# A spectral layer with a routed expert layer on one core: where the next batches' rows are loaded and split, which engine subtracts, and how many buffers the weight parts have

## The chip, the cores and the metric

The kernel runs on one core of a Trainium2 chip. Its engines run at the same time, each through its own queue of instructions in order: TensorE multiplies matrices (PE in the profile, PEld its weight loads), VectorE (DVE), ScalarE (ACT) and GpSimd (POOL) work on tiles, and SyncE (SP) issues transfers between the memory of the chip and the core's own buffers. GpSimd issues the indirect transfers, which send each row to an address that another tile holds. Engines wait for each other through semaphores.

The metric is the time of one execution on the device in microseconds (us), as the median of several runs. Less is better.

## The reference

What is computed, cut to what matters (B = 8 sequences of S = 2496 rows with D = 256, then N = 19968 rows, 8 experts, F = 1024):

```python
X = np.fft.rfft(x, axis=1)
Yr = Xr @ w_r - Xi @ w_i + b_r
Yi = Xr @ w_i + Xi @ w_r + b_i
Y = shrink(Yr, 0.01) + 1j * shrink(Yi, 0.01)     # sign(v) * max(|v| - 0.01, 0)
y = np.fft.irfft(Y, n=2496, axis=1)

x = y.reshape(N, D)
logits = x @ w_gate + modality_bias[modality_id]
e_idx = argmax(logits); gate_w = softmax(logits)[e_idx]
for e in range(8):
    out[e_idx == e] = gate_w * (relu(x @ w1[e]) @ w2[e])
```

## The kernel before

The Fourier transform of length 2496 = 39 x 64 is done in two stages as matrix products, and so is its inverse. To keep enough digits, most operands are split in a high part (rounded) and a low part (the rest), and a product takes three multiplications: high by high, high by low, low by high.

A **batch** is one of the 8 sequences, and `build` (L984) runs them one after the other with hand-written order on TensorE, ScalarE, VectorE and GpSimd (`manual_schedule`, L993). SP is not in that list: the order of the transfers that SP issues is made by a planner from its own estimate of times, under the dependences of the code. A transfer whose buffer isn't free yet holds SP's queue.

A batch has two parts:

- **Ten pairs** (`for p in range(10)`, L1074). Each pair takes two of the 20 frequencies k1 through the second stage (`s2_pair`, L278), the mixing with w_r and w_i (`mix_sums`, L315), the shrinking (`shrink`, L324) and the first stage of the inverse (`is2_pair`, L333). In pair i the loads of pair i+4 are issued (`a_load`, L271), `s2_pair` runs for i+2, mixing and shrinking for i+1 and `is2_pair` for i. ScalarE copies the bias into the accumulator that the next pair's mixing adds to (`mix_bias`, L301).
- **The pivot stage** (`for j in range(J)`, J = 22, L1140): `pivot` (L354) and `is1` (L370) end the inverse and give the rows and their logits. ScalarE and VectorE take turns in copying is1's result (L376, L1148).

Beside these four other jobs are threaded through the same queues:

- **The first stage of batch b+2.** Its rows come in six groups u of four columns (`s1_load`, L209; three transfers on SP each, L226), the tile "x" with **two** buffers. A group gives two chunks c of 512 columns (the last group one): `s1_split` (L231) rounds a chunk to its high part (L240, on ScalarE from batch 2 on) and subtracts to get its low part (L241, on GpSimd for c < 6 from batch 2 on, on VectorE otherwise). `s1_split` also issues the load of its own and of the next group where that hasn't been done. The parts have six buffers each. Groups 0 and 1 are loaded at pairs 2 and 3 (L1102), chunks 0 to 5 are split at the ends of pairs 4 to 9 (L1129), chunks 6 to 10 in the pivot stage (L1145). `s1_chunk` (L244) multiplies them, all in the pivot stage, ScalarE copies the result (L261) and SP stores it to a scratch tensor (L266) that the next batches' `a_load` reads. In batch 0 the same is done for batches 0 and 1 at the start.
- **Routing** of batch b-1's rows (`route`, L456): some twenty small operations, most on VectorE, a few per pair in pairs 0 to 5.
- **Sends** of batch b-1's rows to their experts' regions (`scatter`, L534): 22 indirect transfers of GpSimd, four at each of pairs 6 to 9 (L1107), then one per pivot.
- **The expert weights' parts** (`SplitWeights`, L947): 64 pieces. A `step` (L968) rounds a piece on ScalarE (L977, tile "wh"), subtracts (L978, tile "wl", GpSimd in the pairs and VectorE in the pivot stage), stores both (L979, L980) and loads the next piece (L962, L965, tile "wr" with two buffers). "wh" and "wl" come from the pool w1 and have **one** buffer each. From batch 1 on there is a step in each of pairs 0 to 5 (L1104), in batch 0 in pairs 3 to 7, and at two to four places of each pivot stage (L1150).

Batches 6 and 7 prepare no further batch, and their pivot stages have no chunks.

After the batches `Experts.run` (L901) multiplies the sorted rows in tiles of 256 with their expert's weights (`ffn`, L788); `load_x` and `load_w` bring a tile's rows and weights. Its memory overlays that of the batches.

Of the kernel before, what the change touches and what calls it, by code (L numbers as in the profile page):

```python
# [9 lines left out]
F32 = mybir.dt.float32  # L10
# [13 lines left out]
D = 256  # L24
# [5 lines left out]
P1 = 3 * N1  # L30
# [97 lines left out]
class Attn:  # L128
# [5 lines left out]
    def pools(self, ctx):  # L134
        tc, nb = self.tc, self.nb
        pool = lambda name, bufs, **k: ctx.enter_context(tc.tile_pool(name=name, bufs=bufs, **k))
        self.cp = pool("consts", 1)
        self.w3 = pool("w3", 3)
        self.w4 = pool("w4", 4)

        pool("wq", 1).tile([128, 32], F32, name="wqad")
        self.w6 = pool("w6", 6)
        self.w2 = pool("w2", 2)
        self.w1 = pool("w1", 1)
        self.cl = pool("cl", 1)
        self.ps = pool("ps", 2, space=PSUM)
        self.dr = pool("dr", 2, space=DRAM)
        self.scr = [None] * nb
        self.xt, self.xs = {}, {}
# [59 lines left out]
    def s1_load(self, b, u, end=None, eng=None):  # L209

        nc = self.nc
        eng = eng or nc.sync
        end = end or u + 1
        n = min(4 * end, J) - 4 * u
        xv = self.I["x"][b].rearrange("(a c) d -> a c d", c=N2)
        if b == 0 and u < 5 or b == 1 and u < 3:

            if u == 0:
                self.early = self.x1f[0] if b else self.w1.tile([128, 2 * N2, K1, 2], F32, tag="z", name="x_0")
                if not b:  # L220
                    self.early = self.early.rearrange("p n k r -> p (n k r)")
            xt = self.early[:P1, u * 4 * D:end * 4 * D].rearrange("p (j d) -> p j d", d=D)
        else:
            xt = self.w2.tile([P1, 4, D], F32, tag="x", name=f"x_{b}_{u}")
        for g in range(3):
            ins = eng.dma_start(xt[g * N1:(g + 1) * N1, :n, :], xv[:, GB[g] + 4 * u:GB[g] + 4 * u + n, :])  # L226
        for v in range(u, end):
            self.xt[b, v] = xt[:, 4 * (v - u):4 * (v - u) + 4, :]
        return ins

    def s1_split(self, b, c):  # L231
        nc = self.nc
        u, h = c // 2, c % 2
        for v in (u, u + 1):
            if v < 6 and (b, v) not in self.xt:
                self.s1_load(b, v)
        x = self.xt[b, u][:, 2 * h:2 * h + 2, :].rearrange("p j d -> p (j d)")
        xh = self.w6.tile([P1, 512], F32R, tag="x1h", name=f"x1h_{b}_{c}")
        xl = self.w6.tile([P1, 512], F32R, tag="x1l", name=f"x1l_{b}_{c}")
        (nc.vector.tensor_copy if b == 1 or b == 0 and c % 2 == 0 else nc.scalar.copy)(xh, x)  # L240
        (nc.gpsimd if b > 1 and c < 6 else nc.vector).tensor_sub(xl, x, xh)  # L241
        self.xs[b, c] = xh, xl

    def s1_chunk(self, b, c, ahead):  # L244
# [739 lines left out]
def build(tc, I, out, nb):  # L984
    nc = tc.nc
    with ExitStack() as outer:
        dp = outer.enter_context(tc.tile_pool(name="wsp", bufs=1, space=DRAM))
        wsp = dp.tile([E * 128, 8192], F32, name="wsp")
        with ExitStack() as ctx:
            at = Attn(tc, I, nb)  # L990
            rt = Route(outer, tc, I, at, nb)
            at.pools(ctx)
            ctx.enter_context(tc.manual_schedule(engines={ET.PE, ET.Activation, ET.DVE, ET.Pool}))  # L993
            sw = SplitWeights(tc, I, at.w2, at.w1, wsp)
            at.x1f.append(at.cl.tile([128, J * GC], F32, name="x1b"))
            ld, xs, bs, ss = {}, {}, {}, {}
            last = 10 * nb
# [1 line left out]
            def load(i):  # L999
                if i < last:  # L1000
                    ld[i], ins = at.a_load(*divmod(i, 10))
                    return ins

            def s2(i):
                if i < last:
                    xs[i] = at.s2_pair(*divmod(i, 10), ld.pop(i))
# [13 lines left out]
            def bias(i):  # L1020
                if i < last:
                    bs[i] = at.mix_bias(*divmod(i, 10))

            def ahead(i):
                load(i + 4)
                s2(i + 2)
# [45 lines left out]
            for b in range(nb):  # L1072
                done = b == nb - 1
                for p in range(10):  # L1074
                    i = 10 * b + p
                    due = state == "pe"

                    apart = b == nb - 2 and p == 9
                    if b == 0:
                        if p % 2 == 0 and p < 8:  # L1080
                            with tc.issue_after(ins.ins):
                                if p < 6:
                                    at.table_load("m", p // 2 + 2)
                                at.table_load("q", p // 2 + 1)
                        ins = load(i + 4)
                        s2(i + 2)
                        if p == 0:
                            sw.load()
                            sw.load()
                        if p == 3:  # L1090
                            late = [rt.consts(), at.consts_last()]
                        if p in (3, 6):
                            for g in late:
                                next(g, None)
                        for c in (2 * p + ahead1, 2 * p + ahead1 + 1):
                            if c < 11 and nb > 1:
                                at.s1_chunk(1, c, 2)
                    elif p > 0:
                        ahead(i)
                    if p == 1:  # L1100
                        rt.load_ids(b)
                    if p in (2, 3) and b + 2 < nb:  # L1102
                        at.s1_load(b + 2, p - 2)
                    if p < 6 if b > 0 else 2 < p < 8:  # L1104
                        sw.step(nc.gpsimd)
                    if p > 5:
                        rt.scatter(4)  # L1107
                    if done and 4 < p < 9:
                        bias(i + 2)
                    ending = i == last - 2  # L1110
                    if ending:
                        mix_last(i + 1, 0)
                    else:
                        mix(i + 1, 0 if apart else None)
                    if p < 9 and not (done and p > 4):
                        bias(i + 2)
                    if due:
                        state = next(routing, None)
                    at.is2_pair(b, p, ss.pop(i))
                    if apart:  # L1120
                        mix(i + 1, 1)
                    if ending:
                        mix_last(i + 1, 1)
                    for _ in range(3):
                        if state != "pe":
                            state = next(routing, None)
                    if p == 8:
                        rt.bias(b)
                    if p > 3 and b + 2 < nb:  # L1129
                        at.s1_split(b + 2, p - 4)  # L1130
                if b != nb - 2:
                    for _ in routing:
                        pass

                s1 = [(b + 2, c) for c in range(11)] if b + 2 < nb else []
                if s1:
                    at.s1_chunk(*s1.pop(0), 0)
                    at.s1_chunk(*s1.pop(0), 0)
                pend = []
                for j in range(J):  # L1140
                    rt.scatter(1)
                    pend.append((j, at.pivot(b, j)))
                    chunk = j % 2 == 1 and j != 15
                    if len(s1) > 4 and chunk:
                        at.s1_split(*s1[4])  # L1145
                    if len(pend) > 2:
                        jj, r = pend.pop(0)
                        at.is1(b, jj, *r, nc.scalar.copy if done or jj % 2 else nc.vector.tensor_copy)  # L1148
                    if j in (8, 18) or (b == 0 and j == 13) or (b == nb - 2 and j in (3, 13)):
                        sw.step(nc.vector)  # L1150
                    if s1 and chunk:
                        at.s1_chunk(*s1.pop(0), 0)
                    next(routing, None)
                for _ in routing:
                    pass
                bias(10 * b + 11)
                ahead(10 * b + 10)
                for jj, r in pend:
                    at.is1(b, jj, *r, nc.scalar.copy)
                routing = rt.route(b)  # L1160
                if b == nb - 3:
                    rt.setup_pads()
                    routing = chain(routing, rt.tiles_early())
                if b == nb - 2:
                    rt.fence()
# [38 lines left out]
```

## Time and profile before

| | us |
|---|---|
| median of three runs | 1585.96 |
| lowest and highest of them | 1584.24, 1587.04 |
| the profiled execution's own time | 1588.58 |
| its span, from the first to the last instruction | 1586.8 |
| from the start to the end of the last batch's pivot stage | 667.5 |

The profile is of one execution. A line of the view by groups or of the timeline has the kernel's line (L240 is line 240), the engine, the operation, the tile that is written and those that are read ("x1h<-x"), and their shapes. In the timeline the first two numbers are the start and the duration in us, and what stands in brackets is the idle time of the engine ahead of the instruction, with what ended it. In the view of waits a row has the engine and line that waited, what it waited for, and the total, the number and the longest of these waits in us. In the view by stretches a row has the stretch, its length, the busy time of PE, PEld, DVE, ACT and POOL with their instructions, the granted share of TensorE's clock, the busy share of the DMA engines and GB/s. SPq rows are transfers that SP issues: how long the issue took, not the transfer.

In the profiled execution batch 1 runs its pairs from 143.4 to 186.2 us and its pivot stage to 219.9, and a pair takes 4.5 to 4.9 us.

### The profile page before, as it was taken

What the parts mean: (1) busy time and instruction counts of PE and PEld (TensorE: products, weight loads), DVE (VectorE), ACT (ScalarE), POOL (GpSimd) and SP (SyncE); (2) the same over time, 40 slices, a digit from 0 to 9 for tenths busy, and PEclk for the clock granted to TensorE, in tenths of its full rate; (3) what the DMA queues carried; (4) which work ended last, traced back from release to release, by engine and by line L of the source; (5) the groups of instructions that cost most, each with busy time, mean ns of one, the idle gap of its engine ahead of it and who ended that gap; (6) DMA issues with size and microseconds to landing.
All of it is one profiled execution on the core that took longest, in us unless ns stands there. A gap on an engine that the chain in (4) does not pass through costs nothing. (4 is left out here: it accounts for less than half of the span.)

```text
span 1586.8 us, 34903 instructions
## 1 busy us (share of the span) xinstructions
PE 1510.0 (95%) x12459; PEld 1479.4 (93%) x12459; DVE 695.8 (44%) x1460; ACT 660.9 (42%) x1345; POOL 563.5 (36%) x548
## 2 busy tenths in 40 slices
PE   4889999999999999889999999999999999999998
PEld 2889898989898999889999999999999999999998
DVE  3555555555565666434333333333333333233332
ACT  2466565656565655522323323232233323232232
POOL 0031727272727262523643232222223222222232
PEclk8999999999999999999999999999999999999999
DMA  7866676767676665552442423752225228635541
GB/s 205 260 210 222 200 228 200 229 201 226 203 232 199 214 185 187 149 184 55 99 119 55 150 45 63 244 159 43 52 44 159 45 42 262 233 67 161 146 133 45
DMA packets 290201, 244.44 MB, mean 154 GB/s; under 512 B 208586, under 2 KB 243990, under 8 KB 286207
## 3 DMA queue, kind: packets, MB, share of 16 engines
q1 hardware_dynamic: 271033, 200.60, 43.6%
q0 software_dynamic: 18992, 41.58, 8.0%
q8 instruction: 100, 1.64, 0.4%
q14 instruction: 76, 0.62, 0.1%
HBM read 432.70 MB, written 100.08 MB: 336 GB/s over the span
## 5 line engine op out<-in xcount | busy, mean ns | idle before, releaser
L833 PE MATMUL y<-w,hh 128*128 128x256 f32 x2496 | 437.0, 278 | 7.4 <-DMA w<-wsp 6.9
L803 PE MATMUL h<-xh,w 128*128 128x256 f32 x2496 | 403.5, 278 | 5.1 <-DMA w<-wsp 5.1
L833 PEld LDWEIGHTS y<-w,hh 128*128 128x128 f32 x2496 | 379.3, 188 | 8.3 <-issue 7.0
L833 PE MATMUL y<-w,hl 128*128 128x256 f32 x1248 | 347.5, 278 | 0.1
L803 PEld LDWEIGHTS h<-xh,w 128*128 128x128 f32 x2496 | 339.8, 189 | 5.4 <-issue 5.4
L846 POOL DMA_INDIRECT out<-o,ix x161 | 158.5, 984 | 440.4 <-ACT o L825 402.8
L806 DVE SCALAR_TENSOR_TENSOR hl<-h,hh 128x512 fp32r<-128x512 f32 x312 | 209.5, 689 | 228.6 <-ACT hh L805 225.0
L803 PE MATMUL h<-xl,w 128*128 128x256 f32 x1248 | 245.3, 278 | 0.0
L805 ACT ACTIVATE hh<-h 128x512 fp32r<-128x512 f32 x312 | 178.3, 596 | 152.7 <-PE h L803 152.7
L833 PEld LDWEIGHTS y<-w,hl 128*128 128x128 f32 x1248 | 234.8, 188 | 0.6 <-DVE hl L806 0.3
L321 PE MATMUL mx<-wmix,Xh 128*128 128x256 f32 x1280 | 183.6, 287 | 6.1 <-ACT mx L301 6.1
L803 PEld LDWEIGHTS h<-xl,w 128*128 128x128 f32 x1248 | 189.4, 189 | 0.0
L825 ACT ACTIVATE o<-y,xt 128x256 f32<-128x256 f32 x78 | 37.1, 476 | 347.6 <-PE y L833 347.6
L823 DVE TENSOR_SCALAR o<-y,xt 128x256 f32<-128x256 f32 x78 | 37.8, 484 | 327.3 <-ACT o L825 322.9
L321 PEld LDWEIGHTS mx<-wmix,Xh 128*128 128x128 f32 x1280 | 163.5, 192 | 6.8 <-ACT mx L301 6.3
L783 POOL TENSOR_TENSOR xl<-tr,xh 128x512 fp32r<-128x512 f32 x78 | 100.9, 1294 | 192.8 <-ACT xh L782 192.8
L978 POOL TENSOR_TENSOR wl<-wr,wh 128x512 fp32r<-128x512 f32 x47 | 60.4, 1285 | 253.8 <-ACT wh L977 180.3
L361 PE MATMUL pv<-pv,z 128*120 128x136 f32 x704 | 113.5, 287 | 3.0 <-DVE pl L367 2.5
L361 PEld LDWEIGHTS pv<-pv,z 128*120 128x120 f32 x704 | 101.9, 190 | 10.1 <-DVE pl L367 2.7
L367 DVE TENSOR_TENSOR pl<-pv,ph 120x264 fp32r<-120x264 f32 x176 | 75.3, 431 | 66.5 <-ACT ph L366 62.6
L330 DVE SCALAR_TENSOR_TENSOR s<-mx,u 128x512 f32<-128x512 f32 (+1 forms) x81 | 55.5, 685 | 106.2 <-ACT u L329 106.2
L321 PE MATMUL mx<-wmix,Xl 128*128 128x256 f32 x640 | 101.2, 281 | 0.0
(186 smaller groups left out, 2065.8 us busy)
## 6 DMA issues: line engine op xcount, KB each, us to landing
w<-wsp SPq DMA_DIRECT2D x166, 2048.0 KB
a<-scr SPq DMA_DIRECT2D x80, 256.0 KB
xt<-xs SPq DMA_DIRECT2D x624, 32.0 KB
scr<-ev SPq DMA_DIRECT2D x112, 160.0 KB
x<-in_x SPq DMA_DIRECT2D x108, 156.0 KB
wr<-in_moe_w SPq DMA_DIRECT2D x64, 256.0 KB
wsp<-wh SPq DMA_DIRECT2D x64, 256.0 KB
wsp<-wl SPq DMA_DIRECT2D x64, 256.0 KB
```

The lines of the kernel that those rows point to most:

```text
L321: self.nc.tensor.matmul(ps[i][:, i, :], t[:, 2 * i + c, o:o + 128], self.w[:, wi, c, lo, :], start=False, stop=n == len(ops) - 1, skip_gro ...
L330: nc.vector.scalar_tensor_tensor(s, ps, LAM, u, ALU.add, ALU.min)
L361: nc.tensor.matmul(ps[:PK, c * 128:c * 128 + D // 2 + E], self.z[:, o:o + 3, :, :].rearrange("p n k r -> p (n k r)"), self.pv[:, c, :], st ...
L367: nc.vector.tensor_sub(pl, ps[:PK, :GC], ph)
L783: nc.gpsimd.tensor_sub(xl, tr, xh)
L803: nc.tensor.matmul(ps[:, q, :], w1[:, lo, c, f * 128:(f + 1) * 128], x[:, c, :], start=n == 0, stop=n == 5)
L805: nc.scalar.activation(hh[:, 2 * p:2 * p + 2, :], ps, AF.Relu)
L806: nc.vector.scalar_tensor_tensor(hl[:, 2 * p:2 * p + 2, :], ps, 0.0, hh[:, 2 * p:2 * p + 2, :], ALU.max, ALU.subtract)
L823: nc.vector.tensor_scalar_mul(o[:, s, :], y[s], gate)
L833: nc.tensor.matmul(y[s], lhsT, w2[:, lo, f, :], start=n == 0, stop=n == 23)
L846: ins = self.nc.gpsimd.indirect_dma_start(out=self.out, out_offset=bass.IndirectOffsetOnAxis(ap=ix, axis=0), in_=o, in_offset=None, bounds ...
L978: eng.tensor_sub(lo, raw, hi)
```

## The change

The tile "x" moves to a pool of its own with three buffers. All six groups of batch b+2 are loaded at fixed pairs, 1, 2, 3, 5, 7 and 9, and chunks 0 to 5 are split at the ends of pairs 3 to 8, one pair earlier each. Every low part (L241) is VectorE's. Pairs 6 to 9 issue three sends each instead of four; the others follow one per pivot as before. "wh" and "wl" come from the pool w2 and have two buffers each.

```diff
@@ pools
         self.w6 = pool("w6", 6)
+        self.wx = pool("wx", 3)
         self.w2 = pool("w2", 2)
@@ s1_load
-            xt = self.w2.tile([P1, 4, D], F32, tag="x", name=f"x_{b}_{u}")
+            xt = self.wx.tile([P1, 4, D], F32, tag="x", name=f"x_{b}_{u}")
@@ s1_split
         (nc.vector.tensor_copy if b == 1 or b == 0 and c % 2 == 0 else nc.scalar.copy)(xh, x)
-        (nc.gpsimd if b > 1 and c < 6 else nc.vector).tensor_sub(xl, x, xh)
+        nc.vector.tensor_sub(xl, x, xh)
@@ build
-            sw = SplitWeights(tc, I, at.w2, at.w1, wsp)
+            sw = SplitWeights(tc, I, at.w2, at.w2, wsp)
@@ build, the pairs
                     if p == 1:
                         rt.load_ids(b)
-                    if p in (2, 3) and b + 2 < nb:
-                        at.s1_load(b + 2, p - 2)
+                    if p in (1, 2, 3, 5, 7, 9) and b + 2 < nb:
+                        at.s1_load(b + 2, (1, 2, 3, 5, 7, 9).index(p))
                     if p < 6 if b > 0 else 2 < p < 8:
                         sw.step(nc.gpsimd)
                     if p > 5:
-                        rt.scatter(4)
+                        rt.scatter(3)
...
                     if p == 8:
                         rt.bias(b)
-                    if p > 3 and b + 2 < nb:
-                        at.s1_split(b + 2, p - 4)
+                    if 2 < p < 9 and b + 2 < nb:
+                        at.s1_split(b + 2, p - 3)
```

## The prediction

> **What bounds the kernel now.** The first page gives the span and the busy engine; the view of waits then says what TensorE (PE) waits for.
>
> ```profile
> span 1586.8 us, 34903 instructions
> PE 1510.0 (95%) x12459; PEld 1479.4 (93%) x12459; DVE 695.8 (44%) x1460; ACT 660.9 (42%) x1345; POOL 563.5 (36%) x548
> ...
> PE i L373 <- ACT x L376: 12.8, 4, 5.1
> ...
> PE i L373 <- ACT x1b L376: 8.7, 5, 4.1
> ...
> PE mx L321 <- ACT mx L301: 6.1, 1, 6.1
> PE pv L361 <- DVE pl L367: 2.5, 1, 2.5
> ...
> ACT x1h L240 <- DMA x<-in_x: 30.0, 7, 5.8
> ```
>
> TensorE is the bound, so only its idle time and its slow time can be won: 1586.8 - 1510.0 = 76.8 us idle. 12.8 + 8.7 = 21.5 us of it stand before L373, the first product of is1, behind a ScalarE copy (L376). That copy isn't slow: the last row says that ScalarE itself waited 30.0 us, in seven places, for rows of x. I read one of these places in order of time, in batch 1's pivot stage (TensorE, then ScalarE, GpSimd, SP).
>
> ```profile
> 190.68 0.40 PE L256 MATMUL s<-x1h,c_f 117*120 117x512 f32 x1
> ...
> 193.04 0.40 PE L256 MATMUL s<-x1h,c_f 117*120 117x512 f32 x1
> ...
> 198.89 0.57 PE L373 MATMUL i<-ph,c_g 120*117 120x264 f32 x1 [3.69 <-ACT x L376]
> ...
> 199.69 0.63 PE L256 MATMUL s<-x1h,c_f 117*120 117x512 f32 x1
> ...
> 204.10 0.63 PE L256 MATMUL s<-x1h,c_f 117*120 117x512 f32 x1
> ...
> 197.94 0.62 ACT L240 CAST x1h<-x 117x512 fp32r<-117x512 f32 x1 [4.44 <-DMA x<-in_x]
> ...
> 197.17 1.27 POOL L241 TENSOR_TENSOR x1l<-x,x1h 117x512 fp32r<-117x512 f32 x1
> ...
> 192.82 1.40 SPq L226 DMA_DIRECT2D x<-in_x  x3
> ...
> 198.47 1.16 SPq L226 DMA_DIRECT2D x<-in_x  x3
> ```
>
> Group 4's load leaves SP at 192.82, and its first half is rounded (L240) only at 197.94. ScalarE stands 4.44 us, is1's copies queue behind it, and TensorE idles 3.69. The two x buffers explain the lateness: the sixth load leaves at 198.47, just after GpSimd ends a low part at 197.17 + 1.27 = 198.44. GpSimd gets to that part late, behind its sends.
>
> The stall is paid twice. Two pivots with one chunk take 193.04 - 190.68 = 2.36 us ahead of it and 204.10 - 199.69 = 4.41 right after: slow time loses (4.41 - 2.36) / 4.41 = 46%. The view by stretches, over the six stages that prepare a later batch, shows the granted clock:
>
> ```profile
> 108.47:140.83 32.36, 29.32 (x197) 27.00 (x197) 18.64 (x42) 22.26 (x55) 1.28 (x1) 0.95 0.66 207
> 186.17:219.92 33.75, 30.06 (x197) 27.78 (x197) 17.81 (x41) 22.62 (x54) 17.20 (x17) 0.90 0.72 223
> ...
> 501.87:534.65 32.78, 28.89 (x197) 26.76 (x197) 17.69 (x41) 22.16 (x54) 17.28 (x19) 0.95 0.65 200
> sum 199.26, PE 175.76 PEld 162.50 DVE 107.58 ACT 134.06 POOL 87.21; mean PE 29.29 PEld 27.08 DVE 17.93 ACT 22.34 POOL 14.54
> ```
>
> The third number from the end is the clock: 0.95 in four stages, 0.90 in two, and full or half between. Half clock thus filled 2 x (0.05 x 4 + 0.10 x 2) x 33.2 = 26.6 us (33.2 is 199.26 / 6), and 46% of it, 12.2 us, is lost.
>
> **The change part by part.** *Loads, third buffer, earlier splits.* All six loads of a batch are issued by pair 9, groups 3 to 5 two pairs after the preceding one or two; each needs a buffer whose low parts VectorE ended in the pair before. Group 4 leaves in pair 7, three pairs ahead of the pivots that use it, where it left in their midst. The same 18 transfers move per batch, none is added. I take the stalls before L373 as gone, with their slow time: 21.5 + 12.2 = 33.7 us. The bounds are that, and nothing.
>
> *Low parts on VectorE.* From the groups by line, the ones that VectorE does already:
>
> ```profile
> L241 DVE TENSOR_TENSOR x1l<-x,x1h 117x512 fp32r<-117x512 f32 x52 | 36.6, 707 | 30.9 <-ACT x1h L240 29.1
> ```
>
> Six of each of six batches, 36 subtractions, leave GpSimd and add 36 x 0.707 = 25.5 us to VectorE's queue, in pairs 3 to 8, each between a pair's last routing operation and the next pair's L290. Is there room? Pairs 4 and 5 of batch 1:
>
> ```profile
> 162.97 0.59 ACT L301 COPY mx<-bias 128x512 f32<-128x512 f32 x1
> ...
> 163.82 1.19 PE L321 MATMUL mx<-wmix,Xh 128*128 128x256 f32 x8
> ...
> 163.71 0.68 DVE L348 COPY z<-zs 128x512 f32<-128x512 f32 x1
> ...
> 165.75 0.63 DVE L290 TENSOR_TENSOR Xl<-s,Xh 128x512 fp32r<-128x512 f32 x1
> ...
> 166.41 0.39 ACT L291 ACTIVATE Xh<-s 128x256 fp32r<-128x256 f32 x1 [1.72 <-DVE Xl L290]
> 166.69 0.61 ACT L977 CAST wh<-wr 128x512 fp32r<-128x512 f32 x1
> 167.20 0.69 ACT L329 ACTIVATE u<-mx,nlam 128x512 f32<-128x512 f32 x1
> 167.78 0.60 ACT L301 COPY mx<-bias 128x512 f32<-128x512 f32 x1
> ...
> 168.44 1.20 PE L321 MATMUL mx<-wmix,Xh 128*128 128x256 f32 x8
> ```
>
> This is a closed chain: routing after L348 holds L290 until 165.75, L291 waits for it, then L977, L329 and L301 follow without a break, and L321 starts 0.06 us after L301 ends (168.38). A pair earlier the margin is 163.82 - 163.56 = 0.26. A low part, 0.65 us from start to next start, shifts pair 4's chain past it by 0.4, and pair 5's chain by a second 0.65, so TensorE loses about 0.4 + 0.9 = 1.3 us per batch, in batches 1 to 5: 6.5 us. From pair 6 on there is neither L977 nor routing ahead of L290, and the addition hides. Each loss is under 1 us, and the shortest of the stalls above that has half clock in its stage is 2.5 (L361, stage 0, clock 0.95), so I add no slow time. I take 6.5; the ends are 0 and 25.5 (each low part on the path). ScalarE's own roundings only move one pair forward.
>
> *Two buffers for wh and wl.* Two ScalarE waits hang on a store of the single buffer:
>
> ```profile
> 82.13 0.62 ACT L977 CAST wh<-wr 128x512 fp32r<-128x512 f32 x1 [7.21 <-DMA wsp<-wh]
> ...
> 134.73 0.62 ACT L977 CAST wh<-wr 128x512 fp32r<-128x512 f32 x1 [2.77 <-DMA wsp<-wh]
> ...
> 76.99 0.38 SPq L979 DMA_DIRECT2D wsp<-wh  x1
> ...
> 77.89 0.45 SPq L962 DMA_DIRECT2D wr<-in_moe_w  x1
> ...
> 75.00:91.00 16.00, 9.88 (x67) 9.69 (x66) 3.73 (x7) 5.30 (x10) 3.82 (x3) 0.79 0.71 241
> ```
>
> The second makes the 2.5 us before L361. Its store is then two pieces back: gone, 2.5 us (its slow time is in the 26.6 above). The first makes the 6.1 before L321, and the clock of 0.79 over 16 us adds 2 x 0.21 x 16 = 6.7 us of half clock, 3.1 lost: 9.2 in all. Not all is won: the third piece, one pair (168.44 - 163.82 = 4.6 us) later, needs raw weights that leave SP at 77.89. At the store's own 82.13 - 76.99 = 5.1 us they land at 83.0. ScalarE would want them at 82.13 - 7.21 + 4.6 = 79.5: a wait of 3.5. As 7.21 of ScalarE's wait cost 6.1 of TensorE, 1.1 is hidden: 2.4 remain, and a slow stretch as in the last stage (2 x 0.05 x 32.78 = 3.3 us, 46% of it) 1.5. I take 9.2 - 3.9 = 5.3; the ends are 0 and 9.2.
>
> *Sends.* The 22 sends stay, 12 of them in pairs 6 to 9 instead of 16. GpSimd, freed of the low parts, ends them no later in batches 1 to 5; in 6 and 7, where it had none, a few us later. Expert tile 0's second weights must follow the last send, but stand in SP's queue behind four tiles' row loads: 0.
>
> *The sum.* 33.7 + 2.5 + 5.3 - 6.5 = 35.0 us. The profiled execution took 1588.58 around its 1586.8, so it would take 1553.6; the median of the runs, 1585.96, becomes 1551.
>
> **A rule that speaks against it.** Sends ran beside VectorE's low parts already:
>
> ```profile
> 191.69 0.69 DVE L241 TENSOR_TENSOR x1l<-x,x1h 117x512 fp32r<-117x512 f32 x1
> ...
> 191.86 1.41 POOL L536 DMA_INDIRECT xs<-x1b,si  x1 [0.19 <-issue]
> 193.58 0.99 POOL L536 DMA_INDIRECT xs<-x1b,si  x1 [0.30 <-issue]
> ```
>
> The low part kept its 0.69, the send took 1.41 instead of 0.99. The Trainium skill, "SBUF — State Buffer", section "SBUF: two separate sides", says that a VectorE operation with two SBUF inputs takes the port shared with GpSimd for its whole length, and whoever starts second blocks. By that rule the trace's 0.42 of lengthening is the send's; with the send first, VectorE would wait.
>
> **The rivals.**
> - *The chain has cover* (the margin grows as ScalarE runs ahead): the 6.5 is 0, and 1585.96 - 41.5 = 1544. For it: VectorE is 44% busy. Against: 0.06 us of margin.
> - *The next wait ends just as late.* A load stands behind stores in SP's queue, which is ordered by the planner's own estimate of times, or the last group arrives late: half of 33.7 stays, 1568. For it: 192.82 above was such a queue place. Against: the loads now leave pairs earlier.
> - *VectorE waits for GpSimd's port.* In pairs 5 to 8 sends run back to back. If each of four low parts waits a whole 0.99 and hides half, 6 batches x 4 x 0.5 = 12 us: 1563. Against: the 0.69 above.
> - *SP blocks (slower).* Loads of groups 3 to 5 wait at SP's head for a low part, and scratch loads (L275) stand behind them:
>
> ```profile
> 173.34 4.91 SPq L275 DMA_DIRECT2D a<-scr  x2
> 183.33 1.91 SPq L226 DMA_DIRECT2D x<-in_x  x3
> ```
>
>  Already here SP stands from 178.25 to 183.33, 5.1 us, and TensorE doesn't stall. L275 loads four pairs ahead and is used two pairs later, 9.2 us; with 5.1 to land, 4.1 are free by this estimate. Blocks of 6.9 us (one and a half pairs) would cost 2.8 each, 18 of them 50 us: 1601. It is slower than before from 4.1 + 35.0 / 18 = 6.0 us per block.
> - *The loads stay late*, since SP's order is the planner's and not the code's: only 2.5 + 5.3 - 6.5 = 1.3 is left, 1585.
>
> **How the numbers follow.** Forecast 0.52, cover 0.20, next wait 0.13, port 0.07, loads stay 0.04, SP blocks 0.04. The likeliest gives 1551. The range takes in the cover with the start's whole 9.2 (1541) and reaches over the half-kept stall to the chain's upper end (1551 + 25.5 - 6.5 = 1570); it leaves out the last two cases and some tails. About 0.2%, 3 us, is what a measurement of this kernel can tell from no change. Faster 0.92, same 0.04 (the loads stay), slower 0.04.
>
> **What would show it.** Right: no wait of L373 for L376 above 1 us in stages 0 to 5, their clock at 1.00 and each near 27 us; no L241 on GpSimd; L321 waiting some 0.4 to 0.9 us for L301 in pairs 5 and 6 of batches 1 to 5; the stall at 77.8 shorter, a pair later. Wrong: L240 still waiting for x in the pivots, L284 waiting for the scratch loads, or pairs 4 to 9 longer than 4.6 us throughout.

## The result and the profile after

| | before | after |
|---|---|---|
| median of the runs, us | 1585.96 | 1552.01 |
| lowest and highest | 1584.24, 1587.04 | 1549.88, 1552.37 |
| ratio, with its 95% interval | | 0.978 (0.9764 to 0.9796) |
| the profiled execution's span | 1586.8 | 1550.2 |
| its six pivot stages that prepare a batch | 199.26 | 162.10 |
| its pairs of batches 1 to 5, from pair 0 to pair 9 | 41.62 to 41.74 each | 42.08 to 42.25 each |
| its pairs of batch 0, likewise | 51.96 | 51.59 |

The change makes the kernel 2.2% faster, 1 us from the forecast of 1551. All lines from 143 on are one higher in the changed kernel (L373 is L374, L240 is L241), and one higher again in the kernels below that have a third buffer for the raw weights. First its page, and then its view of waits, with the rows that answer to those shown of before.

```profile
span 1550.2 us, 34912 instructions
PE 1498.1 (97%) x12459; PEld 1468.4 (95%) x12459; DVE 712.4 (46%) x1496; ACT 659.6 (43%) x1345; POOL 517.9 (33%) x512
```

```profile
PEld mx L322 <- ACT mx L302: 7.7, 11, 5.2
...
PE mx L322 <- ACT mx L302: 5.0, 1, 5.0
...
ACT x1h L241 <- DMA x<-in_x: 3.4, 1, 3.4
...
PE i L374 <- ACT x1b L377: 0.3, 2, 0.2
...
PE i L374 <- ACT x L377: 0.2, 1, 0.2
```

TensorE's 21.5 us ahead of is1 have become 0.5, and ScalarE waits 3.4 us for rows of x where it waited 30.0. No row is left of L362 (before's L361) waiting for "pl". The stretches of the six stages, cut as in the prediction:

```profile
106.54:133.59 27.05, 27.05 (x198) 25.24 (x197) 18.62 (x42) 22.07 (x54) 0.00 (x0) 1.00 0.63 202
179.39:206.40 27.01, 27.01 (x197) 25.23 (x197) 17.90 (x41) 21.80 (x53) 13.75 (x13) 1.00 0.76 236
...
471.09:498.09 27.00, 27.00 (x198) 25.23 (x197) 17.92 (x41) 21.76 (x53) 14.18 (x15) 1.00 0.66 200
sum 162.10, PE 162.10 PEld 151.40 DVE 108.24 ACT 130.91 POOL 66.61; mean PE 27.02 PEld 25.23 DVE 18.04 ACT 21.82 POOL 11.10
```

TensorE is busy from end to end at a granted clock of 1.00: 199.26 - 162.10 = 37.2 us are won here. That is more than the whole gain of the spans, 1586.8 - 1550.2 = 36.6. The rest cancels: the pairs of batches 1 to 5 give back 2.5 us (the five differences of their totals), the start up to batch 0's first pair is 1.5 us shorter (it stood at 53.91 us after 55.46, and between 52.9 and 56.3 in all the profiles of this study), and the pairs of batch 0 win 0.4.

### The profile page after: what moved, and what is told of

The parts are those of the page before. It is cut to its first block, busy times and chain, and to the rows that moved or that the text cites. A ratio compares the mean times of both kernels' runs of the same rounds, so it can differ in the third digit from the quotient of the medians.

```text
span 1550.2 us, 34912 instructions
## 1 busy us (share of the span) xinstructions
PE 1498.1 (97%) x12459; PEld 1468.4 (95%) x12459; DVE 712.4 (46%) x1496; ACT 659.6 (43%) x1345; POOL 517.9 (33%) x512
## 5 line engine op out<-in xcount | busy, mean ns | idle before, releaser
L322 PE MATMUL mx<-wmix,Xh 128*128 128x256 f32 x1280 | 182.3, 286 | 5.7 <-ACT mx L302 5.0
L322 PEld LDWEIGHTS mx<-wmix,Xh 128*128 128x128 f32 x1280 | 162.1, 190 | 8.1 <-ACT mx L302 7.7
L362 PE MATMUL pv<-pv,z 128*120 128x136 f32 x704 | 110.3, 282 | 0.5 <-ACT z L349 0.5
L362 PEld LDWEIGHTS pv<-pv,z 128*120 128x120 f32 x704 | 98.7, 185 | 6.7 <-ACT z L349 0.7
L537 POOL DMA_INDIRECT xs<-x1b,si x88 | 91.7, 1042 | 27.1 <-issue 26.1
L322 PE MATMUL mx<-wmix,Xl 128*128 128x256 f32 x640 | 100.7, 280 | 0.0
```

The source lines that it names most:

```text
L322: self.nc.tensor.matmul(ps[i][:, i, :], t[:, 2 * i + c, o:o + 128], self.w[:, wi, c, lo, :], start=False, stop=n == len(ops) - 1, skip_gro ...
L362: nc.tensor.matmul(ps[:PK, c * 128:c * 128 + D // 2 + E], self.z[:, o:o + 3, :, :].rearrange("p n k r -> p (n k r)"), self.pv[:, c, :], st ...
L537: i = self.nc.gpsimd.indirect_dma_start(out=self.xs, out_offset=bass.IndirectOffsetOnAxis(ap=si[:, k:k + 1], axis=0), in_=rows, in_offset= ...
```

## The experiments

Eight kernels were run, some of them more than once, twelve runs in all. They fell on what I call two chips: in two comparisons, that of the result and the next one, the kernel before took 1586 us, in the three others 1638. Whether these are two chips or one in two conditions, the results don't tell; the record gives the same chip number, 0, to one comparison of each kind. Times are compared within one comparison only, and from the slower chip mainly those stretches are read that lie before its trouble begins (the last experiment says where that is).

### The change once more, and low parts off the chain

`c1` is the changed kernel once more, beside the kernel before. `e6` moves the splits and loads of the change and adds a third buffer for the raw weights:

```diff
-                    if p in (1, 2, 3, 5, 7, 9) and b + 2 < nb:
+                    if p in (0, 1, 2, 5, 8) and b + 2 < nb:
...
-                    if 2 < p < 9 and b + 2 < nb:
+                    if p in (2, 3, 6, 7, 8, 9) and b + 2 < nb:
...
+                    at.s1_load(b + 2, 5)
...
+        self.wr = pool("wr", 3)
-            sw = SplitWeights(tc, I, at.w2, at.w2, wsp)
+            sw = SplitWeights(tc, I, at.wr, at.w2, wsp)
...
                             sw.load()
+                            sw.load()
```

> The changed kernel unchanged, beside the kernel before on one chip, because the four runs so far fell on a chip where the kernel before takes 1638 us and not 1586, with idle stretches of 2 to 10 us that end in 'issue' or 'remote'. If the change is worth the same 0.978 on every chip, the ratio is 0.975 to 0.981 here. If those idle stretches hit the changed kernel more (theory of the slower chip), the ratio there is above 0.99, and the profile shows stages of over 30 us with L374 waiting for 'issue', where the first chip's profile shows 27.0 us each. The 4.93 us of pair 4 and the 0.18 us of L529 should be the same on any chip.

> The changed kernel with a third buffer for the raw expert weights (as in e4) and with the six splits at pairs 2, 3, 6, 7, 8, 9 instead of 3 to 8, so that no low part is beside the chain of pairs 4 and 5; loads at pairs 0, 1, 2, 5, 8 and one at the stage's start. Theory (low parts on VectorE cost the pairs of batches 1 to 5 2.5 us in all; the raw weight's landing costs the start about 5): pairs of batches 1 to 5 at about 41.7 us instead of 42.15, the 5.0 us stall at L322 near 82 gone, together 4 to 8 us less than the changed kernel beside it. Rival (any low part on VectorE costs its pair the same wherever it stands): pairs stay at 42.1, 2 to 5 us less. If the load for chunk 10 at the stage's start is late, a stall of 1 to 4 us a stage appears at L260 and the kernel is slower.

The kernel before took 1586.49 us there, the changed one 1551.91, 0.9777 (0.9761 to 0.9793): the same gain. `e6` took 1552.20, 0.9781 (0.9763 to 0.9798): nothing beyond it. Both halves of its theory missed. Its pairs of batches 1 to 5 took 42.11 to 42.21 us. The largest part of the excess over before is pair 4, 4.85 instead of 4.61, since the split of pair 3 still stands ahead of pair 4's L292; the rest is spread over other pairs, some of it from the third raw buffer (see `e9`). Pairs 6 to 8, each with a split, took 4.61 or 4.62. So the rival "a low part costs the same wherever it stands" falls as well: what matters is pair 3. Its stages took 27.0 us, so the load at their start was not late. The pairs of its batch 0 took 51.75 us: the stall of 5.0 us at L322 went, but a new one came, which the profile puts down to rows of x, now loaded in pairs 0 to 2,

```profile
PE s L286 <- DMA x<-in_x: 3.0, 1, 3.0
```

Behind it came 1.5 us for scratch rows (L286) and 2.3 for L303.

### One part of the change at a time

`e1` is the kernel before with `nc.vector.tensor_sub(xl, x, xh)` for every low part and nothing else. `e2`, run three times, is before with the pool "wx", the fixed loads and the earlier splits; its low parts stay GpSimd's.

> The kernel before with one part of the change alone: every low part is VectorE's; two buffers for x, the old places of loads and splits, four sends a pair, one buffer for wh and wl. Theory A (the x loads of the pivot stages left late because GpSimd ended the low parts late, behind its sends): the fifth and sixth loads leave some 10 us earlier in the stage, stages 1 to 5 come down from 32.8-33.9 us to 27-29, and the start's stall and stage 0's 2.5 us stay: 1553 to 1562 us. Theory B (two buffers are the cause, whoever subtracts): the stalls before is1 stay at 3 to 5 us, 1580 us or more. The routing operation L528 should take 0.18 us instead of 0.84 to 0.95, if GpSimd's subtraction beside it was what stretched it.

> The kernel before with the other part alone: third buffer, loads at fixed pairs and splits one pair earlier; low parts of chunks 0 to 5 stay GpSimd's, four sends a pair, one buffer for wh and wl. Theory A (the early loads suffice): no wait of is1 over 1 us, stages 1 to 5 at 27 us, pairs as before (41.7 us per batch, since VectorE gets no low parts there), stage 0 keeps its 2.5 us: about 1553 us. Theory B (GpSimd's queue still holds the low parts of chunks 4 and 5 behind 12 sends, so that the sixth load leaves in the stage): part of the stall stays, 1560 to 1575 us. L528 stays at 0.84 or more in batches 1 to 5.

> The kernel before with the three wx buffers, the loads at fixed pairs and the splits a pair earlier; low parts stay GpSimd's, four sends a pair, one wh and wl buffer; once more, hoping for a chip on which the kernel before takes 1586 us. Theory (the stages' 37 us come from the early loads alone): pivot stages 0 to 5 at 27 us each, 1547 to 1553 us; pairs of batches 1 to 5 near 41.7 us with L529 at 0.84 us or more beside GpSimd; the start's stall is still the store's, near 78. Rival (GpSimd's low parts are part of the stages' delay): the stages stay above 28 us with L374 waiting for chunk copies, 1558 us or more.

> The kernel before with the three wx buffers, loads at fixed pairs and splits a pair earlier; low parts stay GpSimd's, four sends a pair, one wh and wl buffer. Where the kernel before takes 1586 us: if the early loads alone make the stages' 37 us, pivot stages 1 to 5 come to 27.0 us each with no wait of L374 for a copy, stage 0 keeps a stall of about 2 us at L362 near 133 (one wh and wl buffer), the start keeps its 8 us stall at L322 near 76, pairs of batches 1 to 5 stay above 42 us; 1551 to 1558 us. If VectorE's low parts are half of it, stages 1 to 5 stay above 29 us and the time above 1565. Where the kernel before takes 1638 us the ratio is 1.003 as twice already.

All four runs fell on the slower chip: `e1` took 1671.18 us, a ratio of 1.0177 (1.0139 to 1.0215); `e2` took 1643.19, 1643.34 and 1643.31, ratios of 1.003, 1.0038 and 1.0032, each within 1.0006 to 1.0063. So neither part's share of the 37 us can be given for the first chip, and the times expected for it were not put to the test; only the last `e2`'s ratio of 1.003 was foreseen, from the two runs ahead of it. Three things can still be read.

*VectorE's chain.* The next rows are those of one operation of routing, in the views by line of before, the changed kernel, `e1` and the third `e2` (shortest, median and longest in ns):

```profile
L528 DVE TENSOR_SCALAR sm<-sm x8: 178/841/949, 164.7 to 695.8; 117x22 f32<-117x22 f32 x8
```

```profile
L529 DVE TENSOR_SCALAR sm<-sm x8: 177/178/179, 158.1 to 660.1; 117x22 f32<-117x22 f32 x8
```

```profile
L528 DVE TENSOR_SCALAR sm<-sm x8: 178/178/179, 163.2 to 774.2; 117x22 f32<-117x22 f32 x8
```

```profile
L529 DVE TENSOR_SCALAR sm<-sm x8: 178/842/968, 166.2 to 746.5; 117x22 f32<-117x22 f32 x8
```

The same small operation takes 0.84 us or more in batches 1 to 5 where GpSimd has the low parts, and 0.18 where VectorE has them. In each of the five long cases it runs beside a low part on GpSimd; in the three others there is none beside it, and it takes 0.18. The timeline of before, pair 4 of batch 1:

```profile
164.18 1.29 POOL L241 TENSOR_TENSOR x1l<-x,x1h 117x512 fp32r<-117x512 f32 x1
164.67 0.84 DVE L528 TENSOR_SCALAR sm<-sm 117x22 f32<-117x22 f32 x1
```

It ends at 165.51, 0.04 us after GpSimd's subtraction (165.47). This is the rule that the prediction weighed, in the Trainium skill, "SBUF — State Buffer", section "SBUF: two separate sides": a VectorE operation that needs the port shared with GpSimd stands still while GpSimd holds it. The traces agree, and here it speaks for the change: the low part that moves to VectorE gives back 0.84 - 0.18 = 0.66 us at the same place. In the changed kernel's timeline the stretch from the operation ahead of it (L526, now L527) to L290 (now L291) takes 159.03 - 157.71 = 1.32 us, low part included; before it took 165.75 - 164.31 = 1.44 without one. A pair earlier nothing is given back, and the low part (153.66) simply moves L291 by 0.6 us:

```profile
153.55 0.18 DVE L523 TENSOR_TENSOR si<-sl,inv 117x22 int32<-117x22 f32 x1
153.66 0.69 DVE L242 TENSOR_TENSOR x1l<-x,x1h 117x512 fp32r<-117x512 f32 x1
154.27 0.68 DVE L291 TENSOR_TENSOR Xl<-s,Xh 128x512 fp32r<-128x512 f32 x1
...
157.71 0.33 DVE L527 TENSOR_REDUCE sm<-ex 117x22 f32<-117x176 f32 x1
158.07 0.18 DVE L529 TENSOR_SCALAR sm<-sm 117x22 f32<-117x22 f32 x1
...
158.49 0.63 DVE L242 TENSOR_TENSOR x1l<-x,x1h 117x512 fp32r<-117x512 f32 x1
159.03 0.68 DVE L291 TENSOR_TENSOR Xl<-s,Xh 128x512 fp32r<-128x512 f32 x1
```

*Pairs 4 and 5 of batches 2 to 5.* In `e1`, with VectorE's low parts from pair 4 on, they take 4.61 and 4.62 us, where before has 4.61 and 4.53 to 4.66; in `e2`, with GpSimd's from pair 3 on, 4.82 to 4.91 and 4.82 to 5.03; in the changed kernel 4.91 to 4.93 and 4.75 to 4.84. The split at pair 3 is what costs, whoever subtracts. On VectorE its low part stands on pair 4's chain (above). On GpSimd it holds up another operation of the same chain, L518, which takes 0.34 us in the changed kernel; the third `e2`'s timeline:

```profile
160.43 1.30 POOL L242 TENSOR_TENSOR x1l<-x,x1h 117x512 fp32r<-117x512 f32 x1 [0.99 <-ACT x1h L241]
161.00 0.92 DVE L518 TENSOR_TENSOR rk<-rk,oh 117x176 f32<-117x176 f32 x1
```

The split at pair 4 costs nothing that can be seen on either engine: pair 5 takes 4.61 us in `e6` too, which has no split there.

*Waits for rows of x.* ScalarE's total for x is 4.3 us in `e1` (2 waits) and 2.3, 3.0 and 3.2 in `e2`, against 30.0 in before's profile of the first chip. With either part alone hardly any of it is left there. Since the stages are longer on that chip, this doesn't show that one alone would do on the first. SP's timeline says a little more. Group 4 is the one that before waits for. In stages 1 to 5 its first transfer leaves 6.7 us into the stage in before, 2.0 us into it in `e1` (the last at 4.2), and 9.7 to 11.3 us ahead of it in `e2`. Where nothing holds it up, ScalarE takes the group's first half at 7.2 us (the changed kernel); in before it took it 5.1 us after the first transfer had left and 4.1 after the last (192.82 and 193.84 to 197.94). By this estimate the early loads have room to spare, and VectorE's low parts alone would be just in time or about 1 us late.

### One buffer for the weight parts, or three for the raw ones

`e3`, run twice, gives wh and wl one buffer again (`SplitWeights(tc, I, at.w2, at.w1, wsp)`). `e4`, run twice, is the changed kernel with the third raw buffer alone (the last two hunks of the diff above). `e7` loads batch 0's rows for batch 2 later:

```diff
+                    if b == 0 and p in (5, 6, 7, 9):
+                        at.s1_load(2, (5, 6, 7, 9).index(p))
...
+                        for c in {7: (0,), 8: (1, 2), 9: (3, 4, 5)}.get(p, ()):
+                            at.s1_split(2, c)
```

> The changed kernel with one buffer for wh and wl again. Theory A (the second buffer only moved the start's wait from the store of a piece to the load of the third piece, and removed stage 0's stall of 2.5 us with its slow clock): start as long as now within 2 us, stage 0 longer by 2.5 to 4 us: about 1555 us. Theory B (as the prediction had it, the second buffer is worth 5 us at the start and 4 in stage 0): about 1561 us.

> The changed kernel with one buffer for wh and wl again. Theory by the DMA engines (they move 351 GB/s in 80 to 90 us of the changed kernel, so the start is bound by bytes, and the second buffer only moves the wait): 0 to 2 us slower than the changed kernel, stall total between 76 and 92 us at 5 to 8 us. Rival (the second buffer removed a wait of 7 us that would be back): 5 to 7 us slower.

> The changed kernel with three buffers for the raw weights (wr) and three pieces loaded at batch 0's first pair instead of two. Theory A (ScalarE's 6.8 us wait at the start is for the third piece's load, which leaves SP only after the first piece is split): the wait goes and TensorE's 5.0 + 0.8 us with the slow clock behind it, some 8 us: 1544 us. Theory B (the wait passes on to the fourth piece, one pair later): 1548 to 1552 us.

> The changed kernel with a third raw weight buffer, so that all three pieces are loaded ahead. Theory by the DMA engines: the stall of 5.0 us at L322 near 82 goes, but one of about the same size comes at L286 on a<-scr, since the same bytes are still due by then; 0 to 2 us less than the changed kernel. Rival (the wait for the raw piece alone costs it): 4 to 6 us less, 1546 to 1548.

> The changed kernel; in batch 0 alone the next first stage's rows are loaded at pairs 5, 6, 7 and 9 (two more at the end of pair 9) and split at pairs 7 to 9 instead of loaded from pair 1 and split from pair 3. Theory by the DMA engines: three loads of 0.47 MB, 1.4 MB or 4 us at 350 GB/s, leave the stretch up to 87 us, and the stall between 76 and 92 us shrinks from 5.8 to 1 to 3 us; 2 to 5 us less, 1547 to 1550. Rival (the raw piece's own latency, not the bytes ahead of it, makes the stall): stall unchanged at 5 to 6 us, time 1551 to 1553, or slower if the six low parts in three pairs cost VectorE's chain 1 us or the stage's chunks wait for their rows.

All on the slower chip, and all far from the expected times: 1693.32 and 1700.64 us for `e3`, 1686.96 and 1686.59 for `e4`, 1692.04 for `e7`, ratios of 1.0339, 1.0367, 1.0293, 1.0298 and 1.0341. Batch 0 and its stage come before any send, so they can be read.

*The stall of stage 0.* With one buffer, `e1`, `e2` and `e3` all have it, 1.8 to 2.8 us in six profiles; with two it is in none of seven (the changed kernel twice, `e4` twice, `e6`, `e7`, `e9`). In the second `e3` (timeline):

```profile
128.96 0.37 SPq L980 DMA_DIRECT2D wsp<-wh  x1
...
133.75 0.62 ACT L978 CAST wh<-wr 128x512 fp32r<-128x512 f32 x1 [2.96 <-DMA wsp<-wh]
...
135.56 1.26 PE L362 MATMUL pv<-pv,z 128*120 128x136 f32 x4 [2.71 <-DVE pl L368]
```

The chain is that of the prediction: the store of wh, ScalarE in order behind it, then TensorE. Stage 0 as a whole takes 31.0 and 31.5 us in `e3`, 29.3 to 32.4 in before, `e1` and `e2`, and 27.0 to 27.6 in the kernels with two buffers. So some 4 of the 37.2 us belong to the second buffer, the slow time behind the stall included.

*The start.* The time from pair 0 to pair 9 of batch 0, in us:

| kernel | pairs of batch 0 |
|---|---|
| one buffer, late loads: before, `e1` | 51.96, 51.80 |
| one buffer, early loads: `e2` three times, `e3` twice | 53.68, 54.40, 53.47, 53.78, 54.10 |
| two buffers, early loads: the changed kernel twice | 51.59, 53.16 |
| two buffers, batch 0's loads late: `e7` | 51.49 |
| and three raw buffers: `e4` twice | 49.71, 46.73 |

Early loads cost the start about 2 us, and the second buffer wins about that back. Against the changed kernel, `e3` thus loses 1 to 2 us at the start and 4 in stage 0, as the first theory A had it; the sum, some 6, is that of the second run's rival. What ends the wait with two buffers is the raw piece, in the changed kernel's timeline:

```profile
78.35 0.40 SPq L963 DMA_DIRECT2D wr<-in_moe_w  x1
...
85.46 0.62 ACT L978 CAST wh<-wr 128x512 fp32r<-128x512 f32 x1 [6.80 <-DMA wr<-in_moe_w]
...
86.56 0.59 ACT L302 COPY mx<-bias 128x512 f32<-128x512 f32 x1
87.20 2.07 PE L322 MATMUL mx<-wmix,Xh 128*128 128x256 f32 x8 [5.00 <-ACT mx L302]
```

85.46 - 78.35 = 7.1 us from issue to use, and TensorE restarts at half speed (2.07 us for eight products that take 1.2 elsewhere). With the piece asked for ahead (`e4`) this wait is gone in both runs, and what is left are 3.3 and 1.7 us for scratch rows. So the piece is asked for too late; that is shown.

Why it then needs 7 us and not the store's 5.1 stays open. One theory is that the DMA engines were full (busy share 1.02 and 351 GB/s from 80 to 90 us, where before has 0.68 and 242). `e7` was to test it and doesn't, as SP's timeline there shows:

```profile
66.88 0.36 SPq L227 DMA_DIRECT2D x<-in_x  x1
...
67.76 0.84 SPq L227 DMA_DIRECT2D x<-in_x  x2
...
73.84 0.75 SPq L227 DMA_DIRECT2D x<-in_x  x2
...
76.11 0.82 SPq L227 DMA_DIRECT2D x<-in_x  x2
...
77.45 0.80 SPq L227 DMA_DIRECT2D x<-in_x  x2
...
78.76 0.82 SPq L963 DMA_DIRECT2D wr<-in_moe_w  x1
```

SP's order is the planner's, so the rows leave before the pairs that name them: these are nine transfers, three groups, ahead of the raw piece, as many as in the changed kernel and later than there. While the piece was under way, from 80 to 85 us, the busy share was 1.03 (1.06 in the changed kernel); it fell only after 85. The stall, 6.25 us, was no shorter. The raw piece was used at 85.46 us in the changed kernel, at 85.53 in its second profile and at 85.80 in `e7`, though it had left SP at 78.35, 80.42 and 78.76. That leaving 2 us earlier brought nothing speaks for full engines and against a fixed time of landing; it doesn't prove it.

### Both repairs in one kernel

`e9` is the changed kernel with the third raw buffer, splits at pairs 4 to 9 and loads to fit:

```diff
-                    if p in (1, 2, 3, 5, 7, 9) and b + 2 < nb:
+                    if p in (1, 2, 3, 6, 8) and b + 2 < nb:
...
-                    if 2 < p < 9 and b + 2 < nb:
-                        at.s1_split(b + 2, p - 3)
+                    if p > 3 and b + 2 < nb:
+                        at.s1_split(b + 2, p - 4)
+                        if p == 9:
+                            at.s1_load(b + 2, 5)
```

> The changed kernel with a third raw weight buffer (as e4) and the splits back at pairs 4 to 9 on VectorE, loads at pairs 1, 2, 3, 6, 8 and after the last split. Theory 1, from two traces: with splits from pair 4 on, VectorE's low parts cost the pairs nothing (4.61 us for pairs 4 and 5 in the kernel before with VectorE low parts), so pairs of batches 1 to 5 come to 41.5 to 41.7 us instead of 42.15, 2 to 3 us in all. Theory 2: the start's stall is the wait for the raw piece, and with all three pieces ahead it shrinks from 5.8 to 1 to 3 us. Both: 1544 to 1549 us where the kernel before takes 1586. Rival (the start is bound by bytes): stall total between 76 and 95 us stays at 5 to 7 us and the time is 1549 to 1552.

The slower chip again: 1683.63 us, 1.027 (1.0236 to 1.0303). In the parts before the sends both theories hold: pairs 4 and 5 take 4.61 or 4.62 us in all five batches, and batch 0's pairs 45.43 us, 6.2 less than in the changed kernel. Two pairs grew, pair 1 from 4.63 to 4.73 and pair 3 from 4.56 to 4.64, in `e4` as well, so that belongs to the raw buffer. Seven pairs of a batch come to 32.7 us instead of 33.0, only 0.3 less. By these sums `e9` would be the best version where the kernel before takes 1586 us; it never ran there, so that is not shown.

### What the slower chip does

The stretches of stages 0 and 1 of `e9`:

```profile
102.55:129.81 27.26, 27.26 (x200) 25.44 (x199) 19.29 (x42) 22.41 (x56) 0.00 (x0) 1.00 0.65 212
182.54:223.44 40.90, 31.69 (x200) 28.88 (x199) 18.25 (x42) 22.70 (x55) 12.48 (x13) 0.83 0.54 170
```

Stage 0 is that of the first chip (the changed kernel's, cut alike, has 27.29). Stage 1, with the same products and 13 sends on GpSimd, takes 13.6 us longer, with the DMA engines less busy (0.54). The timeline of `e9` shows where it begins, with the first sends of all:

```profile
158.10 1.20 POOL L538 DMA_INDIRECT xs<-x1b,si  x1 [0.21 <-POOL wl L980]
...
163.15 8.53 SPq L277 DMA_DIRECT2D a<-scr  x2
...
168.68 0.99 POOL L538 DMA_INDIRECT xs<-x1b,si  x1 [0.31 <-issue]
171.17 0.69 ACT L331 ACTIVATE u<-mx,nlam 128x512 f32<-128x512 f32 x1 [6.28 <-remote]
...
172.40 2.08 PE L323 MATMUL mx<-wmix,Xh 128*128 128x256 f32 x8 [5.23 <-ACT mx L303]
```

Nine sends follow each other at 1.3 us. Some 7 us after the first, ScalarE stops for 6.28 us at a wait that the profile puts down to "remote" (it knows no instruction that ended it), and TensorE after it; they go on 1.5 us after the run's last send ends (168.68 + 0.99). SP stands in the same time: the row of 8.53 us is two transfers, whose issue takes 0.39 us each, and the second leaves only at 171.29. On the first chip the same place, under the same run of nine, has no such wait (second profile of the changed kernel):

```profile
170.65 0.69 ACT L330 ACTIVATE u<-mx,nlam 128x512 f32<-128x512 f32 x1 [0.99 <-PE mx L322]
...
172.37 5.00 SPq L276 DMA_DIRECT2D a<-scr  x2
175.26 0.69 ACT L330 ACTIVATE u<-mx,nlam 128x512 f32<-128x512 f32 x1 [0.99 <-PE mx L322]
```

I counted TensorE's gaps above 0.7 us from 100 to 800 us, and how many lie in a run of five or more sends (up to 3 us behind its last). `e9`: 31 in runs, 92 us in all, and 2 outside, 2 us. `e4`, `e3` and `e7`: 89 to 95 us in runs. `e1`: 63. The last `e2`: 53. The changed kernel on the first chip, with the same runs of 9 and 13: 5 (second profile) and 2. The kernel before sends in runs of four to six in batches 1 to 5, since GpSimd subtracts in between (in batches 6 and 7, which have no low parts, in runs of 12 and 10). `e2` still does so in its pairs: its pairs 6 and 7 of these batches take 4.5 to 4.8 us there, where in `e3`, `e4`, `e7` and `e9` pair 7 takes 11.4 to 12.7. So the gaps go with the long runs of sends; that the runs make them is not shown, since no kernel spread out its sends and changed nothing else. What delays the waits isn't in the profile, and I did not find it: the sends themselves take 0.99 us on both chips. The changed kernel itself was not timed on the slower chip and there is no profile of the kernel before from there. As four near copies of it came out 2.7 to 3.7% slower than before there, I would expect it to lose on such a chip; that is argued, not shown.

## Why the prediction was right

- **Loads, third buffer, low parts: the stages.** Forecast 33.7 + 2.5 = 36.2 us, measured 37.2. The signs came as named: clock 1.00, 27 us a stage, no wait of L374 above 0.2. Which part did it on the first chip is open: with each alone the waits for x were nearly gone, but only on the slower one; by the times at which group 4 leaves, the early loads do most.
- **Low parts on VectorE: the chain, 6.5 us.** Right in its place, pairs 4 and 5 of batches 1 to 5 (its list of signs calls them 5 and 6), wrong in size: 2.5. The weight loads show the waits for L302: 0.27 to 0.34 us in pair 4, near the 0.4, but at most 0.17 in pair 5 instead of 0.9. So the rival in which the chain has cover and costs nothing came nearer than the 6.5. The term of 0.4 + 0.9 = 1.3 per batch left out that GpSimd's low part held up L528 by 0.66 us on the same chain: 1.3 - 0.66 = 0.64 would have been near the 0.36 to 0.63 by which the five batches grew. That rule was weighed, but for VectorE's low parts against sends, not for what the old low parts did to routing. The prediction's own row, L290 at 165.75 so late after L348 at 163.71, contained it.
- **The start, 5.3 us.** Wrong: 0.4 in the profiled run, and 1.2 lost in the second one (53.16 against 51.96). The step that failed is the raw piece's landing, taken at the store's 5.1 us; it took 7.1 in the profiled run, and in the second, where it left 2 us later, 5.1. The early loads, which the prediction gave no price at the start, cost it about 2. The stall came a pair later, as forecast, but of 5.0 us and 0.8 more for scratch rows instead of 2.4.
- **Two buffers in stage 0, 2.5 us.** Right, and shown on the slower chip and the first by seven profiles with the stall (before, `e1`, `e2`, `e3`) and seven without. With its slow time it is worth about 4.
- **Sends at no cost.** Right on the chip of the result: the expert part took 919.5 us before and 919.6 after. The part that mattered elsewhere, that GpSimd without its low parts sends nine in a row, was not weighed at all.
- **The sum.** 1551 against 1552.01 is partly luck. Two errors cancel: 4.0 us too dear for the chain, 4.9 too kind at the start. And the profiled execution of before took 2.6 us more than the median, that of the changed kernel took its median, so that the parts above add up to the 36.6 us between the spans where the medians differ by 34.0. The rivals "next wait just as late", "port" and "SP blocks" each needed a loss of 12 us or more, and no trace of the first chip has one; the loads didn't stay late either (group 4 leaves 11.9 us ahead of stages 1 to 5).

## What to carry to other kernels

When work moves between VectorE and GpSimd, look in the old trace for operations that GpSimd stretched: one of 0.18 us that takes 0.84 is part of the balance. A second buffer removes a wait only down to the next transfer of the same chain; work out when that one is issued before counting the whole wait as won. A change that frees an engine also lets what is left on it bunch together, and whether the bunch costs anything can depend on the chip or its condition: time such a change more than once, and on more than one chip.

## What the runs showed of the hardware that was not expected

- The same kernel took 1586 us in some comparisons and 1638 in others (medians of 7 and 13 runs). In `e9`, one of the slower ones, the expert part takes 913.6 us against 919.6 in the changed kernel on the faster chip, so it isn't slower throughout: the loss lies in the batches, and in the kernels profiled there inside runs of indirect sends.
- There, waits between engines stretch to 2 to 10 us while GpSimd issues sends back to back, and SP stands as well (7.7 us between the two transfers at 163.15 and 171.29), with the DMA engines half idle (busy share 0.55 from 158 to 182 us of `e9`).
- A VectorE operation with a single input (L528, 117x22) was held up by GpSimd's subtraction from 0.18 to 0.84 us, and one with two (L518, 117x176) from 0.34 to 0.92.
- A short idle time can be enough to halve TensorE's clock. In before's stage 0 the one idle time of the first stretch below is 2.46 us, and the whole next stretch ran at 0.50; in `e1` 1.81 us had the same effect.

```profile
133.29:136.70 3.41, 0.94 (x8) 0.72 (x7) 1.04 (x2) 1.95 (x5) 0.00 (x0) 1.00 0.77 280
136.70:140.11 3.41, 3.41 (x17) 3.41 (x17) 1.21 (x3) 1.27 (x4) 0.00 (x0) 0.50 0.81 276
```
